# Block-masked attention and a mixture of experts: the row maxima masked in PSUM, the row tails loaded per batch, the token rows stored by two transfers

## Chip, core and metric

The kernel runs on one core of a Trainium2 chip. The metric is the device time of one execution in microseconds (us). The engines are named as in the profile: PE is TensorE (PEld its weight loads), DVE is VectorE, ACT is ScalarE, POOL is GpSimd, SP is SyncE, which here issues most of the DMAs.

## What is computed

```
q, k, v: (8, 8, 576, 64)        # batch, heads, sequence, head dimension
scores = q @ k.T / sqrt(64)
scores = where(pos_q // 64 >= pos_k // 64, scores, -1e9)
attn   = softmax(scores)         # row maximum taken off first, 1e-9 added to the sum
x      = (attn @ v) as (4608, 512)
# router: cosine of x with 8 expert vectors, divided by tau; argmax picks the expert
out[i] = gate[i] * (relu(x[i] @ w1[e]) @ w2[e])      # e = expert of token i
```

The mask is by blocks of 64: a query of block b sees keys of blocks 0 to b.

## The kernel before

**Two stages.** The first 410 us or so are attention with the routing of each batch beside it. The rest is the experts: 36 to 43 slots of 128 tokens, gathered from a DRAM buffer `xbuf`, each through two layers with split (high and low) fp32r products. The change touches the first stage alone.

**Attention by pairs.** Work goes by pairs of heads: 8 batches of 4 pairs, 32 pairs. The two heads of a pair lie on partitions 0 to 63 and 64 to 127. For each pair there are generators of small steps: `prep` (turn q and k on PE, split them into high and low parts on ACT and DVE), `maxes` (row maxima of the scores), `scores` (the scores again, keys on the partitions, then exp), `values` (attention times v, and the sums), `finish` (turn back, divide, write `xrow`), `route` (the router of a whole batch) and `loads` (DMAs three pairs ahead).

**What sets the order.** Nothing is scheduled by the compiler: `run` reads a string for each pair and advances one generator by one step for each letter (`m` maxes, `s` scores, `v` values, `f` finish, `p` prep, `r` route, `l` loads). `FIRST` has the strings of pairs 0 to 4, `FINAL` those of pairs 27 to 31, `STEADY` the one string of the 22 pairs between. Each engine then runs its own instructions in exactly that order.

**The row maxima.** `maxes` takes the queries in five chunks `c` of 128, shifted by 64, so that the lower 64 partitions hold block 2c-1 and the upper 64 block 2c. For each chunk and head one matmul (L326) writes the scores of all keys that the chunk may see into a buffer of the PSUM pool `ps_m` (four buffers, shared by the two heads of `maxes`, by `scores` and by a few small users). DVE then reduces them. As the last 64 keys are seen by the upper half alone, there are two reductions: L332 on 128 partitions over the keys that both halves see, L334 on the upper 64 partitions over the last 64 keys. Chunk 4 is cut in two. L336 takes the least of the (negated) partial maxima, PE turns it (L296, `nmr`), ACT copies it (L342) and SP writes it as a row of `qa` (L344), from where `scores` adds it by a matmul with `ka`.

**Loads and stores.** `load_rows` fills a buffer of 5 x 128 rows for a pair: one DMA for each head's 512 full rows and one for the last 64 rows of both heads (L204). `route` stores the finished rows of a batch to `xbuf` with five DMAs, one for each block of 128 (L593), and for the last two batches through `store`.

Of the kernel before, what the change touches and what calls it, by code (L numbers as in the profile page):

```python
# [18 lines left out]


FIRST = (
    "rmrrmmrmmmmrmsmmpprmrmrmrrmmkrsssmsrrpprrmrmrspsmrmvlssssmrmsrvmvrspmvvvmrsmrkmsssvsmrmvrkssssvrsprpmmvsmrmrmmvpsvmrrm",
    "srfrrmslfrfrprrrmsrprfmfsmmrrvrvprrrsrrrvmrrrvmrmmrpmmrrvvrpmrvvrlr",
    "vmpsfrvrrmrvrrrrrsrmrrrsmmrmrvsfrpmrrsffmrmpsrrrssmrmpfrrsprfssmmvvmrssmmssvmvvmmmrsrsvvvsmpsvmsmvvrrplmsv",
    "msrmrrrfsrrrrrrrfpmrffsrmmprrmrrmrsffsmrrrsvrmmrpvsvrrmmvrprrsrrf",
    "mmsmrprrmsvsrvvrrvmsmmpvrssrrsrrrvrvrmmvrrmsrrmrfmsfrfrlrrsmsfrrpsrrrsrpfsmpfmss",
)
# [3 lines left out]
FINAL = (
    "vrvvvmmmmmrppvvvpvsmsrmmspvrvmsrrsrmvmrrsrrrrrsrmmmvrsffrrrsfmrsmrrrprsrmmmsmsrffsrm",
    "srlvfrrmvvmmrrmmrrmrvvrmvrmmrsvrpsmvrsmrmpmmvrrsrpvvrssmrrspvmmrsmrmrfrfrsrpfffrpsrsssvfsrrsmmmvvvvlsmlpvsvl",
    "rmvpsvmmpmssrsmrvvrrmsmvfspmrsrfffsrfmmmvrmpvmmrrrssrrrrmprsmmmvmrrssvvmrvrvmvmvmrsmrsrsrvmmmfrsvmrsmsv",
    "rrfprlrmsfmsmrmfsmmfsmffrsssvrrsvvvrvsfrrrrrvvssrf",
    "rrssrvrsrrrrsrvsvvrsrrrvrrrrrsssffrsfrrrsfsrsfrrrffrrr",
)


# [9 lines left out]
def kernel(  # L49
# [145 lines left out]
    psum_t = psum.enter_context(ExitStack())  # L195
    ps_t = pool(psum_t, "ps_t", 1, space=PSUM)

    nat = [[op.tile([P, NJ, 2, D], F32, name=f"{nm}n{i}") for nm in "qk"] for i in range(2)]
    vo = [rt.tile([P, NJ, 2, D], F32, name=f"vo{i}") for i in range(NV)]

    def load_rows(a, src, b, h0):
        for hh in range(2):
            nc.sync.dma_start(a[:, 0:NJ - 1, hh, :], src[b, h0 + hh, 0:S - 64, :].rearrange("(j p) d -> p j d", p=P))
        nc.sync.dma_start(a[0:64, NJ - 1, :, :], src[b, h0:h0 + 2, S - 64:S, :].rearrange("h p d -> p h d"))  # L204

    def load(n):
# [59 lines left out]
    en = const.tile([E, 1], F32, name="en")
# [1134 lines left out]
```

## Time and profile before

| What | us |
|---|---|
| median of three timed runs | 872.85 (871.83 to 873.13) |
| the profiled execution | 872.06 |
| its span, first to last instruction | 870.3 |
| PE busy | 834.4 (96%) |
| DVE busy | 685.9 (79%) |
| ACT busy | 419.6 (48%) |
| POOL busy | 442.0 (51%) |

The shares are means over both stages. Matmuls are pipelined and a matmul that waits for its buffer can still count as busy, so that PE's 96% is not a share of useful work. In the expert stage PE is busy without a break; in attention both PE and DVE are busy most of the time.

### The profile page before, as it was taken

The numbers are of one execution on the slowest core, as the hardware profiler recorded it, in microseconds if no ns is written. First come the engines' busy times: TensorE is split into PE (matmuls) and PEld (weight loads), VectorE is DVE, ScalarE is ACT, GpSimd is POOL, SyncE is SP. The second block draws the span as 40 slices with busy tenths as digits, with TensorE's granted clock in tenths as the row PEclk, the third lists the DMA queues.
The fourth block names the chain that finished last, engine by engine and source line by source line (L and its number), as shares of the span: only waits on it lengthen the run. The fifth ranks groups of instructions, "written<-read, shape, count | busy, mean of one in ns | idle before, by whom it ended". The sixth has DMA issues, their size and how long they took to land. (4 is left out here: it accounts for less than half of the span.)

```text
span 870.3 us, 23939 instructions
## 1 busy us (share of the span) xinstructions
PE 834.4 (96%) x7147; PEld 650.0 (75%) x7147; DVE 685.9 (79%) x1829; ACT 419.6 (48%) x991; POOL 442.0 (51%) x509
## 2 busy tenths in 40 slices
PE   8998999999999999999999999999999999999997
PEld 3666776677767766767787888778888888888885
DVE  6787888888888888885886777887777777788772
ACT  2445646556565655566555535554453333442332
POOL 5345465664667465747332837878383111472111
PEclk8799999999999999999999999999999999999999
DMA  3542454343524343331756444745353111012111
GB/s 86 116 115 59 98 134 100 110 110 90 133 60 123 84 128 73 87 77 61 263 190 214 145 147 147 210 150 182 113 163 131 50 51 51 27 46 64 43 40 48
DMA packets 142995, 94.02 MB, mean 108 GB/s; under 512 B 119981, under 2 KB 121597, under 8 KB 142828
## 3 DMA queue, kind: packets, MB, share of 16 engines
q1 hardware_dynamic: 135372, 71.84, 29.6%
q0 software_dynamic: 7456, 20.26, 7.3%
q8 instruction: 67, 1.10, 0.5%
q14 instruction: 100, 0.82, 0.3%
HBM read 72.71 MB, written 19.71 MB: 106 GB/s over the span
## 5 line engine op out<-in xcount | busy, mean ns | idle before, releaser
L1061 DVE STREAM_TRANSPOSE pt<-h 32x256 f32<-32x256 f32 x528 | 240.8, 456 | 18.3 <-ACT h L1033 0.3
L378 ACT ACTIVATE pT<-psm 128x288 f32<-128x288 f32 (+3 forms) x320 | 122.4, 432 | 89.3 <-PE psm L370 83.8
L332 DVE TENSOR_REDUCE nmx<-psm 128x1 f32<-128x320 f32 (+4 forms) x320 | 130.2, 422 | 37.7 <-PE psm L326 31.2
L815 POOL TENSOR_TENSOR ring_l<-raw,ring_h 128x1024 f32 (+1 forms) x49 | 116.4, 2408 | 36.0 <-ACT ring_h L810 18.4
L1075 POOL DMA_INDIRECT out_dram<-y,outi x36 | 37.2, 1034 | 176.9 <-ACTq L964 129.9
L355 POOL TENSOR_TENSOR pS<-pT 128x448 f32<-128x448 f32 x62 | 69.5, 1146 | 96.9 <-ACT pT L378 82.2
L370 PE MATMUL psm<-qh,kh 64*128 64x288 f32 (+4 forms) x384 | 97.0, 344 | 16.6 <-DVE nmx L334 14.3
L355 POOL TENSOR_TENSOR pS<-pS,pT 128x320 f32<-128x320 f32 (+1 forms) x186 | 106.6, 592 | 11.1 <-ACT pT L378 6.1
L1013 PE MATMUL py<-ring_h,hh 128*128 x272 | 109.5, 402 | 0.8 <-ACT hh L1067 0.8
L1013 PE MATMUL ph<-ring_l,xh 128*128 x280 | 109.1, 390 | 1.1 <-POOLq L976 1.1
L1013 PE MATMUL ph<-ring_h,xh 128*128 x280 | 109.1, 390 | 0.6 <-ACTq L964 0.6
L1013 PE MATMUL py<-ring_l,hh 128*128 x272 | 106.3, 391 | 0.0
L404 PE MATMUL psb<-pT,vo 128*64 128x256 f32 (+1 forms) x868 | 104.5, 367 | 0.3 <-DVE lgh L477 0.3
L1033 ACT ACTIVATE h<-ph 128x512 f32<-128x512 f32 x70 | 42.5, 608 | 99.4 <-DVE pt L1061 61.7
L1013 PE MATMUL py<-ring_h,hl 128*128 x272 | 88.8, 389 | 0.0
L1069 DVE TENSOR_TENSOR hl<-pt,hh 128x512 fp32r<-128x512 f32 x66 | 42.5, 687 | 57.6 <-ACT hh L1067 54.2
L370 PEld LDWEIGHTS psm<-qh,kh 64*128 64x128 f32 x384 | 54.8, 189 | 39.5 <-PE psm L326 21.1
L326 PE MATMUL psm<-kh,qh 64*128 64x320 f32 (+4 forms) x384 | 77.8, 354 | 4.5 <-DVE nmx L334 3.7
L334 DVE TENSOR_REDUCE nmx<-psm 64x1 f32<-64x64 f32 x320 | 71.9, 227 | 9.8 <-PE psb L296 3.8
L370 PE MATMUL psm<-ql,kh 64*128 64x288 f32 (+4 forms) x384 | 79.2, 321 | 0.0
L1013 PE MATMUL ph<-ring_h,xl 128*128 x280 | 74.9, 389 | 0.0
L404 PEld LDWEIGHTS psb<-pT,vo 128*64 128x64 f32 x868 | 53.8, 136 | 28.2 <-issue 9.8
(271 smaller groups left out, 1714.9 us busy)
## 6 DMA issues: line engine op xcount, KB each, us to landing
raw<-in_moe_w_dram SPq DMA_DIRECT2D x64, 512.0 KB
qn<-in_q_dram SPq DMA_DIRECT2D x64, 128.0 KB
kn<-in_k_dram SPq DMA_DIRECT2D x64, 128.0 KB
vo<-in_v_dram SPq DMA_DIRECT2D x64, 128.0 KB
xbuf<-xrow SPq DMA_DIRECT2D x24, 260.0 KB
xbuf<-xrow SPq DMA_DIRECT2D x1, 1040.0 KB
qn<-in_q_dram SPq DMA_DIRECT2D x32, 32.0 KB
kn<-in_k_dram SPq DMA_DIRECT2D x32, 32.0 KB
```

The costliest lines, as they stand in the source:

```text
L326: nc.tensor.matmul(mx[hh][:, 0:e - a], qh[i][hd[hh], c * P:(c + 1) * P], kh[i][hd[hh], a:e], start=True, stop=True)
L332: nc.vector.tensor_reduce(m[:, r, u:u + 1], mx[hh][:, 0:w], axis=AX.X, op=ALU.max, negate=True)
L334: nc.vector.tensor_reduce(m[64:P, r, 1:2], mx[hh][64:P, w:e - a], axis=AX.X, op=ALU.max, negate=True)
L355: nc.gpsimd.tensor_tensor(o, pT[0:r, P:S] if t == 1 else o, pT[0:r, off[t]:off[t] + w], op=ALU.add)
L370: nc.tensor.matmul(st[hh][:, o:o + c1 - c0], kk[hd[hh], t * P:(t + 1) * P], qq[hd[hh], 64 + c0:64 + c1], start=(x == 0), stop=(x == len(te ...
L378: nc.scalar.activation(pT[:, f:f + o], st[hh][:, 0:o], AF.Exp, scale=scale)
L404: m = nc.tensor.matmul(ob[hh * D:(hh + 1) * D, b0:b0 + q1 - c0], a[:, t, hh, :], pTs[hh][0][:, f0:f0 + q1 - c0], start=(t == 0), stop=(t = ...
L815: return eng.tensor_tensor(piece(ring_l, to, c, half), raw[i][:, c * CW:(c + 1) * CW], piece(ring_h, to, c, half).bitcast(F32), op=ALU.sub ...
L1013: m = nc.tensor.matmul(out, ac, slots[g]["w", i](r, c * n + off), start=(u == 0 and c == 0), stop=(c == nk - 1 and u == len(turns) - 1))
L1033: nc.scalar.activation(h[:, f:f + 512], ph, AF.Relu)
L1061: nc.vector.transpose(pt[32 * j:32 * j + 32, :, 32 * i:32 * i + 32], h[32 * i:32 * i + 32, :, j, :])
L1069: nc.vector.tensor_tensor(sets["hl"][u], pt[:, 4 * u:4 * u + 4], sets["hh"][u].bitcast(F32), op=ALU.subtract)
```

## The change

It has three parts, and new strings for all pairs. In `maxes`, after the two score matmuls of a chunk, two matmuls of 64 columns (a constant tile `mk`) add -1e30 to the lower 64 partitions in the last 64 columns. One reduction of 128 partitions over all columns then stands for L332 and L334. The last 64 rows of q, k and v of all eight heads of a batch are loaded by one DMA each into tiles of their own (`ends_n`, `ends_v`, two of each). The rows of every batch are stored by `store`, with two DMAs. With the tail tiles zeroed on all 128 partitions, POOL's sum of the last block runs on 128 partitions.

```
 STEADY = (
-    "vvrvvmmmmvvmrpmpmsvsvmmsvsmrsspvmmvmrmmsvfmmrprlfrssfsmssfrpsmfmssrpf",
+    "vrvvvmmmmvvrmmpmspsvmmvspvmmlrsvvsmsrvmrsfmmrmmmffprssssfrsspmfmssrfp",
...
-    def load_rows(a, src, b, h0):
+    def load_rows(a, end, src, n):
+        b, h0 = n // NP, 2 * (n % NP)
+        if h0 == 0:
+            nc.sync.dma_start(end[b % 2][0:64], src[b, :, S - 64:S, :].rearrange("h p d -> p h d"))
         for hh in range(2):
-            nc.sync.dma_start(a[:, 0:NJ - 1, hh, :], src[b, h0 + hh, 0:S - 64, :].rearrange("(j p) d -> p j d", p=P))
-        nc.sync.dma_start(a[0:64, NJ - 1, :, :], src[b, h0:h0 + 2, S - 64:S, :].rearrange("h p d -> p h d"))
+            nc.sync.dma_start(a[:, :, hh, :], src[b, h0 + hh, 0:S - 64, :].rearrange("(j p) d -> p j d", p=P))
...
+    def init_mk(eng):
+        eng.memset(mk.bitcast(F32), 0.0)
+        for g in range(2):
+            eng.memset(mk[g * D:g * D + 1, 0:64].bitcast(F32), 1.0)
+            eng.memset(mk[g * D:g * D + 1, P:P + 64].bitcast(F32), -1.0e30)
...
                 nc.tensor.matmul(mx[hh][:, 0:e - a], qh[i][hd[hh], c * P:(c + 1) * P], kh[i][hd[hh], a:e],
-                                 start=True, stop=True)
+                                 start=True, stop=e <= 2 * c * 64 or c == 0)
+            if e > 2 * c * 64 and c > 0:
+                for hh in range(2):
+                    nc.tensor.matmul(mx[hh][:, e - a - 64:e - a], mk[hd[hh], 0:P], mk[hd[hh], P:P + 64], start=False, stop=True)
             yield "fine"
             for hh in range(2):
-                r, w, u = hh * NJ + c, min(e, 2 * c * 64) - a, 2 if a else 0
-                if w > 0:
-                    nc.vector.tensor_reduce(m[:, r, u:u + 1], mx[hh][:, 0:w], axis=AX.X, op=ALU.max, negate=True)
-                if a + w < e:
-                    nc.vector.tensor_reduce(m[64:P, r, 1:2], mx[hh][64:P, w:e - a], axis=AX.X, op=ALU.max, negate=True)
+                r, u = hh * NJ + c, 1 if a else 0
+                nc.vector.tensor_reduce(m[:, r, u:u + 1], mx[hh][:, 0:e - a], axis=AX.X, op=ALU.max, negate=True)
...
-        if b < B - 2:
-            for j in range(NJ):
-                r0 = b * S + 1 + j * P
-                r = min(P, S - j * P)
-                nc.sync.dma_start(xbuf[r0:r0 + r, :], xrow[0:r, j, :])
-                yield
-        else:
-            store(b, xrow, 0 if b < B - 1 else (NP - 1) * P, RW)
-            yield
+        store(b, xrow, 0 if b < B - 1 else (NP - 1) * P, RW)
+        yield
```

**DVE in a middle pair.** The rows go from the reductions ahead of `ql` (the low part of the next q) to the last reductions of the pair; `rin` and `xrow` are the division of the pair before. Before:

```order
L332 TENSOR_REDUCE nmx_193<-psm 128x1
L334 TENSOR_REDUCE nmx_193<-psm 64x1
L316 TENSOR_TENSOR ql_180<-pst,qh_177 128x2x5x64
L332 TENSOR_REDUCE nmx_193<-psm 128x1
L334 TENSOR_REDUCE nmx_193<-psm 64x1
...
L334 TENSOR_REDUCE nmx_193<-psm 64x1 x2
L464 TENSOR_SCALAR rin<-psb 128x4x2
L466 TENSOR_SCALAR rin<-psb 128x2
L467 RECIPROCAL rin<-rin 128x5x2
L334 TENSOR_REDUCE nmx_193<-psm 64x1
L470 TENSOR_TENSOR xrow<-psb,rin 128x5x128
```

Now:

```order
L351 TENSOR_REDUCE nmx_199<-psm 128x1 x6
L333 TENSOR_TENSOR ql_186<-pst,qh_183 128x2x5x64
L351 TENSOR_REDUCE nmx_199<-psm 128x1 x6
L481 TENSOR_SCALAR rin<-psb 128x4x2
L483 TENSOR_SCALAR rin<-psb 128x2
L484 RECIPROCAL rin<-rin 128x5x2
L487 TENSOR_TENSOR xrow<-psb,rin 128x5x128
```

Twelve reductions stand where there were twenty, and the last of them has moved ahead of `rin`.

**PE in a middle pair,** from the 448-key chunk to the 320-key chunk, with the scores of 288 columns (`kh`, `kl`, `ka`) between. Before:

```order
L326 MATMUL psm<-kh_182,qh_176 128x448 x2
L370 MATMUL psm<-qh_178,kh_184 128x288 x2
L370 MATMUL psm<-ql_181,kh_184 128x288 x2
L370 MATMUL psm<-qh_178,kl_187 128x288 x2
L370 MATMUL psm<-qa_190,ka 128x288 x2
L404 MATMUL psb<-pT,vo_157 64x192 x2
L404 MATMUL psb<-pT,vo_157 64x64 x2
L370 MATMUL psm<-qh_178,kh_184 128x288 x2
...
L326 MATMUL psm<-kh_182,qh_176 128x320 x2
```

Now:

```order
L343 MATMUL psm<-kh_188,qh_182 128x448 x2
L347 MATMUL psm<-mk 128x64 x2
L387 MATMUL psm<-qh_184,kh_190 128x288 x2
...
L421 MATMUL psb<-pT,vo_157 64x192 x2
L421 MATMUL psb<-pT,ve_165 64x64 x2
L343 MATMUL psm<-kh_188,qh_182 128x320 x2
L347 MATMUL psm<-mk 128x64 x2
L387 MATMUL psm<-qh_184,kh_190 128x288 x2
```

The 320-key chunk has moved ahead of the second group of scores; each of four chunks has a pair of `mk` matmuls behind it; the rest of the pair stands as before.

**PE in the first pair,** where the maxima of pair 1 (`kh_183`, now `kh_189`) meet the scores of pair 0. Before:

```order
L326 MATMUL psm<-kh_183,qh_177 128x320 x2
L326 MATMUL psm<-kh_183,qh_177 128x256 x2
L326 MATMUL psm<-kh_183,qh_177 128x448 x2
L370 MATMUL psm<-qh_176,kh_182 128x288 x2
...
L326 MATMUL psm<-kh_183,qh_177 128x320 x2
L296 MATMUL pst<-ident,qn_153 128x64 x10
L326 MATMUL psm<-kh_183,qh_177 128x192 x2
```

Now:

```order
L343 MATMUL psm<-kh_189,qh_183 128x448 x2
L347 MATMUL psm<-mk 128x64 x2
L343 MATMUL psm<-kh_189,qh_183 128x320 x2
L347 MATMUL psm<-mk 128x64 x2
L343 MATMUL psm<-kh_189,qh_183 128x192 x2
...
L343 MATMUL psm<-kh_189,qh_183 128x64 x2
L387 MATMUL psm<-qh_182,kh_188 128x288 x2
```

All chunks of pair 1 now stand ahead of the first scores of pair 0.

## Rows read from the trace of the kernel before

**Rows 1.** Page, part 1: busy us, share of the span, instructions

```profile
PE 834.4 (96%) x7147; PEld 650.0 (75%) x7147; DVE 685.9 (79%) x1829; ACT 419.6 (48%) x991; POOL 442.0 (51%) x509
```

**Rows 2.** Windows: length, busy by engine (x count), PE clock, DMA share, GB/s

```profile
3.00:6.00 3.00, 3.00 (x17) 1.14 (x15) 1.07 (x2) 0.35 (x1) 1.06 (x7) 1.00 0.59 131
...
12.00:15.00 3.00, 1.96 (x6) 1.13 (x6) 2.79 (x12) 0.00 (x0) 2.87 (x5) 0.77 0.00 0
...
18.00:21.00 3.00, 2.63 (x16) 1.22 (x12) 1.84 (x4) 0.69 (x1) 0.00 (x0) 0.50 0.47 108
...
30.00:33.00 3.00, 2.99 (x26) 1.80 (x27) 1.08 (x3) 2.20 (x7) 2.09 (x2) 0.89 0.01 2
...
103.00:301.00 198.00, 187.29 (x2525) 138.84 (x2527) 168.65 (x544) 113.63 (x320) 118.73 (x172) 1.00 0.42 105
```

**Rows 3.** One line's instructions, 103 to 301: count, ns, first and last start

```profile
L444 ACT COPY su<-psb x17: 319/319/325, 103.4 to 300.5; 128x192 f32<-128x192 f32 x17
```

**Rows 4.** Waits, 103 to 301: who <- whom, total us, times, longest

```profile
PEld psm L370 <- PE psm L326: 13.3, 33, 0.5
DVE nmx L332 <- PE psm L326: 11.8, 16, 1.1
PE psm L370 <- DVE nmx L334: 8.8, 34, 0.5
...
PEld psm L370 <- PE psm L370: 5.3, 12, 0.5
...
PEld psm L370 <- PE psm L541: 2.5, 4, 0.6
```

**Rows 5.** Groups by shape, DVE reductions: busy us, mean ns, idle before

```profile
L334 DVE TENSOR_REDUCE nmx<-psm 64x1 f32<-64x64 f32 x320 | 71.9, 227 | 9.8 <-PE psb L296 3.8 <-PE psm L326 0.9 <-PE psm L370 0.3
...
L332 DVE TENSOR_REDUCE nmx<-psm 128x1 f32<-128x384 f32 x64 | 35.7, 558 | 3.1 <-PE psm L326 1.2
...
L332 DVE TENSOR_REDUCE nmx<-psm 128x1 f32<-128x320 f32 x64 | 28.5, 487 | 24.6 <-PE psm L326 24.5
L332 DVE TENSOR_REDUCE nmx<-psm 128x1 f32<-128x256 f32 x64 | 26.9, 421 | 3.9 <-PE psm L326 2.7
...
L332 DVE TENSOR_REDUCE nmx<-psm 128x1 f32<-128x192 f32 x64 | 22.6, 353 | 3.8 <-PE psm L326 2.8
...
L332 DVE TENSOR_REDUCE nmx<-psm 128x1 f32<-128x128 f32 x64 | 18.6, 290 | 2.3 <-PE psm L370 0.4
```

**Rows 6.** Timeline of one middle pair: start, us, instruction [idle before <- releaser]

```profile
188.26 0.23 DVE L334 TENSOR_REDUCE nmx<-psm 64x1 f32<-64x64 f32 x1
188.52 0.42 DVE L332 TENSOR_REDUCE nmx<-psm 128x1 f32<-128x256 f32 x1
...
193.84 0.17 DVE L336 TENSOR_REDUCE nmr<-nmx 128x10 f32<-128x30 f32 x1
...
195.71 0.53 PE L326 MATMUL psm<-kh,qh 64*128 64x320 f32 x4
...
196.15 1.15 DVE L332 TENSOR_REDUCE nmx<-psm 128x1 f32<-128x320 f32 x3 [0.98 <-PE psm L326]
...
197.73 0.45 PE L326 MATMUL psm<-kh,qh 64*128 64x448 f32 x2
```

**Rows 7.** Timeline, same pair: pairs of 64-column matmuls behind one another

```profile
193.61 0.24 PE L370 MATMUL psm<-qh,kh 64*128 64x64 f32 x2
193.66 0.31 PE L370 MATMUL psm<-ql,kh 64*128 64x64 f32 x2
193.77 0.31 PE L370 MATMUL psm<-qh,kl 64*128 64x64 f32 x2
193.88 0.31 PE L370 MATMUL psm<-qa,ka 64*128 64x64 f32 x2
```

**Rows 8.** Timeline of the start: the first turn of k

```profile
6.48 0.64 PE L296 MATMUL psb<-ident,kn 64*128 64x64 f32 x10
```

More of the change, by code (lines that the diff above doesn't have):

```diff
@@ L21 @@
 FIRST = (
[L22 to L26, printed above, removed]
+    "mmmrmmmmmmmmmmpmmmrrrrlmprrsmmpmrkrskrrsrsssprspsssvpmssrrmvvvmkpsmrvsvsrmrvmrvpprvmmmlmvmvmsmvpfmrfssmmrrsmpmsfrsssssffsrrvvsmpsmpmmrrrmrvvpsv",
+    "rpmrrrsmmmvvrrrrrvmvmsmrrsrmvmssmmrrprssrvfrr",
+    "rlrmmrrvprmsrmsrfmfmmfsrprmsrprmrssssrmfprfvrrrrvvsrmvrrprmrvmrsmrsr",
+    "fsvsrmrrsmvmmvrmsmpmvsrrmrrpvrvsvprmrlrrmrssffmrrrsmspsrfffmmrrvsmrsrvfmmvmrmvrpvmvmssprmrrrrvvrrss",
+    "mvrrrrmrrrrrrlrrmvrsrrvmmrsrvmsfmmfrsmrrrmrrprffrfrsrpssrsrsrspsf",
 )
 STEADY = (
-    "vvrvvmmmmvvmrpmpmsvsvmmsvsmrsspvmmvmrmmsvfmmrprlfrssfsmssfrpsmfmssrpf",
+    "vrvvvmmmmvvrmmpmspsvmmvspvmmlrsvvsmsrvmrsfmmrmmmffprssssfrsspmfmssrfp",
 )
 FINAL = (
[L32 to L36, printed above, removed]
+    "vmmvrvvprmmvmvmrpvvvrpmsppmrmrprsvvvslssrrsrrrfrrfsfmfsmrmrmfrsmrmrrsssmmmvmsrmmrmrvprsmsmrpvmrmmvmvvvrvmmvssvvrmsrmrrsvs",
+    "frfrfrssprfrrrfmpmrsrrmssmfvvprmmsrmrslrrpvsprrmrrrrpmfrrmvrvsmsrvvvmrrrmsvsmsr",
+    "mrrvrrrmrvrsvffrmspsmmrrsfmrpsssffsmmmmpvvmmmsvsmrmrvrv",
+    "mrmmrmmssrrvvrvsvrsrlpsmf",
+    "rmmvfmmlmrrvssrssvrrrmsmmfrsmfmmmmfsffrsfssssrrvvfrvvvvvrvsrrrrslsvsrsssrvvsrrrrrsrrvsfsffrsssrrfsfrffr",
 )
@@ L196, with rows @@
     ps_t = pool(psum_t, "ps_t", 1, space=PSUM)
-    nat = [[op.tile([P, NJ, 2, D], F32, name=f"{nm}n{i}") for nm in "qk"] for i in range(2)]
-    vo = [rt.tile([P, NJ, 2, D], F32, name=f"vo{i}") for i in range(NV)]
-    def load_rows(a, src, b, h0):
+    nat = [[op.tile([P, NJ - 1, 2, D], F32, name=f"{nm}n{i}") for nm in "qk"] for i in range(2)]
+    vo = [rt.tile([P, NJ - 1, 2, D], F32, name=f"vo{i}") for i in range(NV)]
+    ends_n = [[op.tile([P, H, D], F32, name=f"{nm}e{i}") for nm in "qk"] for i in range(2)]
+    ends_v = [rt.tile([P, H, D], F32, name=f"ve{i}") for i in range(2)]
+    def load_rows(a, end, src, n):
+        b, h0 = n // NP, 2 * (n % NP)
+        if h0 == 0:
+            nc.sync.dma_start(end[b % 2][0:64], src[b, :, S - 64:S, :].rearrange("h p d -> p h d"))
         for hh in range(2):
-            nc.sync.dma_start(a[:, 0:NJ - 1, hh, :], src[b, h0 + hh, 0:S - 64, :].rearrange("(j p) d -> p j d", p=P))
-        nc.sync.dma_start(a[0:64, NJ - 1, :, :], src[b, h0:h0 + 2, S - 64:S, :].rearrange("h p d -> p h d"))
+            nc.sync.dma_start(a[:, :, hh, :], src[b, h0 + hh, 0:S - 64, :].rearrange("(j p) d -> p j d", p=P))
+    def rows(a, end, n, j):
+        return a[n % len(a)][:, j] if j < NJ - 1 else end[n // NP % 2][:, 2 * (n % NP):2 * (n % NP) + 2]
     def load(n):
-        for a, src in zip(nat[n % 2], (q, k)):
-            load_rows(a, src, n // NP, 2 * (n % NP))
+        for u, src in enumerate((q, k)):
+            load_rows(nat[n % 2][u], [e[u] for e in ends_n], src, n)
     def load_v(n):
-        load_rows(vo[n % NV], v, n // NP, 2 * (n % NP))
+        load_rows(vo[n % NV], ends_v, v, n)
     ctx.enter_context(tc.manual_schedule())
@@ L216 @@
     for i in range(2):
-        for a in nat[i]:
-            nc.gpsimd.memset(a[64:P, NJ - 1], 0.0)
+        for a in ends_n[i]:
+            nc.gpsimd.memset(a[64:P], 0.0)
     exf = xpool.tile([P, NJ, RW], F32, name="xrow").rearrange("p j w -> p (j w)")[0:NJ + 1, 0:2 * SP]
@@ L235 @@
     NB = S // 64
-    nmx = [rt.tile([P, 2 * NJ, 3], F32, name=f"nmx{i}") for i in range(2)]
+    nmx = [rt.tile([P, 2 * NJ, 2], F32, name=f"nmx{i}") for i in range(2)]
+    mk = op.tile([P, P + 64], F32R, name="mk")
     nmr = [rt.tile([P, P], F32, name=f"nmr{i}") for i in range(2)]
@@ L261, in zeros @@
         nc.gpsimd.memset(enT, 0.0)
-        for i in range(NV):
-            nc.gpsimd.memset(vo[i][64:P, NJ - 1], 0.0)
+        for i in range(2):
+            nc.gpsimd.memset(ends_v[i][64:P], 0.0)
     enT = rt.tile([P, NP, 32], F32, name="enT")
@@ L306, in prep @@
             for j in range(NJ):
-                halves_turned(lambda g: pt[:, g * 512 + j * 64:g * 512 + j * 64 + 64], nat[n % 2][u][:, j, :, :])
+                halves_turned(lambda g: pt[:, g * 512 + j * 64:g * 512 + j * 64 + 64],
+                             rows([a[u] for a in nat], [e[u] for e in ends_n], n, j).rearrange("p h d -> p (h d)"))
             yield "fine"
@@ L351, in add @@
     def add(ps, t, pT):
-        r, w = (P if t < NJ - 1 else 64), S - P * t
-        o = ps[0:r, P * (t - 1):S - P]
-        nc.gpsimd.tensor_tensor(o, pT[0:r, P:S] if t == 1 else o, pT[0:r, off[t]:off[t] + w], op=ALU.add)
+        w = S - P * t
+        o = ps[:, P * (t - 1):S - P]
+        nc.gpsimd.tensor_tensor(o, pT[:, P:S] if t == 1 else o, pT[:, off[t]:off[t] + w], op=ALU.add)
     def scores(n):
@@ L391, in values @@
         pTs = made[n]
-        a, o = vo[n % NV], oe[n % 2]
+        o = oe[n % 2]
         ob = ps_b.tile([P, 1024], F32, name="psb") if n < NPAIR - 1 else ps_t.tile([P, 1024], F32, name="pst")
@@ L403, in values @@
                     f0 = off[t] + c0 - t * P
-                    m = nc.tensor.matmul(ob[hh * D:(hh + 1) * D, b0:b0 + q1 - c0], a[:, t, hh, :],
+                    m = nc.tensor.matmul(ob[hh * D:(hh + 1) * D, b0:b0 + q1 - c0], rows(vo, ends_v, n, t)[:, hh, :],
                                          pTs[hh][0][:, f0:f0 + q1 - c0], start=(t == 0), stop=(t == last))
@@ L719 @@
     init(nc.vector, 0)
+    init_mk(nc.vector)
     init_a(nc.vector, ka)
```

## The prediction, made before the changed kernel was run

> **What bounds the kernel now.** I read the page's busy line first: PE 96%, DVE 79% [rows 1]. Both are means over two stages, and the change touches attention alone, so I took the windows next. In the 198 us of even attention from 103 to 301, PE is busy 187.29 and DVE 168.65 [rows 2]. Seventeen copies of one kind, one for each pair, start from 103.4 to 300.5 [rows 3]: 197.1 us over 16 intervals, 12.32 us for a pair, in which DVE works 168.65 / 16.07 = 10.5 us. To see which of the two waits for the other I read the waits of the same stretch [rows 4]. PE's matmuls of the scores wait for reductions of L334 34 times, 8.8 us. That counts only the time in which no earlier matmul is still shown as running. The weight loads in front of those matmuls stand still longer: 13.3 us behind a chunk of maxima (L326), 5.3 behind scores and 2.5 behind the routing, each time since the pool's next PSUM buffer has not yet been reduced. Together that is 21.1 us, or 21.1 / 16 = 1.32 us a pair. DVE in turn waits for PE 16 times, 11.8 us, once a pair, for the first chunk of the next pair.
>
> The timeline shows the loop that these make [rows 6]. DVE ends the maxima with L336 at 193.84; PE turns the result, does the values it has queued, and only then the next first chunk (195.71), whose reduction starts at 196.15. That is 2.31 us from L336 to the first reduction. The remaining 12.32 - 2.31 = 10.01 us DVE is at work nearly without a pause. So in attention DVE sets the pace over most of a pair and PE over the rest.
>
> **The change, part by part.**
>
> *Reductions.* In a pair L334 runs ten times (x320 for 32 pairs), 227 ns each [rows 5], and 0.26 us from its start to the next one's start (188.26 to 188.52) [rows 6]. Two of the ten (chunk 0) stay, as 128 x 64. Eight go, and the reductions beside them become 64 columns wider. From 256 to 320 columns that costs 487 - 421 = 66 ns, from 320 to 384 it costs 71, from 128 to 192 it costs 63 [rows 5]; I take 67. The relief is 8 x (0.26 - 0.067) = 1.54 us of DVE a pair, or 8 x (0.227 - 0.067) = 1.28 if the gap behind an instruction is kept.
>
> [...]
>
> *Mask matmuls.* Four chunks each get two matmuls of 64 columns, one for each half of the rows. Such pairs stand in the scores of the last key block: starts 193.66, 193.77, 193.88 [rows 7], 0.11 us for a pair of them. They have the tile form of the chunks (64 rows, 128 columns), so I take that price: 4 x 0.11 = 0.44 us of PE a pair. From below the bound is 0.05 (the start at 193.61 to the next at 193.66), from above 0.11 plus nothing that a row shows.
>
> [...]
>
> *What a pair gains.* I work it out in two ways. By the waits: the 1.32 us that PE stands still for DVE's buffers go, since each buffer is held shorter, and 0.44 is paid: 0.88. By the loop: DVE's 10.01 becomes 10.01 - 1.54 = 8.47, plus 2.31 is 10.78. But DVE now gets ahead of PE at one place. The three reductions that begin at 196.15 end at 197.30; in the new order all four of chunk 4 end about 1.64 us after 196.15, at 197.79. The 448-key chunk stands behind values and the turning of q on PE and comes out at 197.73 + 0.45 [rows 6], 0.11 later with its mask: 198.29. So DVE is idle there for 0.5 us: 11.28, a gain of 1.04. I take 0.96 between the two.
>
> *Steady and edge pairs.* The order of the 22 middle pairs is nearly the old one: the 320-key chunk ahead of the second group of scores, and the reduction of chunk 0 ahead of `rin` instead of behind it (it held back the scores of the last two key blocks). So the full gain stands for 22 pairs: 21.1 us. The ten pairs of the first and last strings are ordered quite differently now; I take half, 4.8 us, with 0 and 9.6 as ends.
>
> *Tails.* Bytes are the same over a batch, so the DMA share of 0.42 [rows 2] stays. SP issues six loads a pair instead of nine, plus three a batch. The tails of q and k now stand ahead of the first rows: 2 x 96 KB more before the first k is complete. At 131 GB/s [rows 2] that is 1.5 us at most; nothing, if the filling matmuls ahead of the first turn of k (6.48 [rows 8]) cover it. I take 0.7 us.
>
> *Stores, zeros, constants.* Two stores a batch for five. On SP the pair of stores now stands ahead of the next `qa` row, which scores wait for. The gate that the store needs is written by DVE ahead of the pair's last reductions, and the row only after them, so the store does not hold it: 0. The memsets of `mk` fall where DVE is busy 1.07 of 3 us [rows 2]. POOL's last sum on 128 partitions hides in POOL's 118.73 of 198.
>
> *The sum.* 21.1 + 4.8 - 0.7 = 25.2 us off the profiled execution's 872.06: 846.9. The median of the runs is 0.8 above that execution, so I forecast 847.7.
>
> **The rivals.**
>
> *DVE's loop alone.* If PE is always ready, the 0.5 us of new idle does not come: 1.54 a pair, 22 x 1.54 + 10 x 0.77 - 0.7 = 40.9, 832 us. For it: DVE's only wait in [rows 4] is the one a pair. Against: PE needs its own time for values and turns between chunks.
>
> *The buffers take it back.* Four PSUM buffers are two pairs of them. With the 320-key chunk moved ahead, it must wait until the 448-key chunk is reduced, which comes behind a chunk 0.5 us late. If half of the 1.32 us comes back in this way, a pair gains 0.66 - 0.44 = 0.22: 5.9 - 0.7 = 5.2 us, 867.6. If a little more comes back, the time is unchanged.
>
> *PE is the bound (slower).* PE is shown as busy 95% of even attention. If the idle weight loads are covered by matmuls still streaming, then taking DVE's work away frees nothing and eight more matmuls a pair are simply added: 32 x 0.44 = 14.1, with the start 887.6. It decides where less than 0.44 us of PE's waits goes for a pair. The 8.8 us of idle matmul time are only 0.55 us a pair, so it is not far; against it speaks that DVE has 10.5 of 12.32 us of work and that the buffers are held by it.
>
> [...]
>
> **How the numbers follow.** Forecast 0.50; DVE's loop alone 0.10; the buffers 0.18; PE the bound 0.12; the clock 0.05; no change, where gain and price meet, 0.05. A measurement of this kernel tells about 0.2% (1.7 us) from no change. Faster: 0.50 + 0.10 + 0.05 and all but 0.01 of the buffers, 0.82. Within 0.2%: 0.06. Slower: 0.12. The range reaches up to the buffers' 868 and down to 833, which takes in half of DVE's loop alone (its edge pairs gain anything from 0 to all); 0.17 is left out.
>
> **What would show it.** In the profile after: 12 reductions a pair, 128 x 448 near 0.62 us; DVE busy near 9.2 us a pair; the distance from pair to pair 11.2 to 11.5 us; PE's waits on DVE down to a third; `mk` matmuls 0.11 us a pair of them; a short wait of DVE for the 448-key chunk; the expert stage as before. It is wrong if the pair is above 12 us, if the wait in front of the 320-key chunk is long, or if the first pairs take longer than before.

## The result, and the profile after

The changed kernel takes 840.26 us in the median of four runs (837.98 to 841.55), the kernel before on the same chip 872.99 (871.83 to 873.22). The ratio is 0.9625, with an interval of 0.9602 to 0.9648: 32.7 us or 3.7% faster. The forecast was 847.7, with 833 to 868 as its range; sign and mechanism held, the gain is 7.4 us larger than forecast. The profiled execution takes 839.99 us and spans 838.3.

Part 1 of the page, as in [rows 1] (busy us, share of the span, instructions):

```profile
PE 821.3 (98%) x7403; PEld 658.0 (78%) x7403; DVE 621.7 (74%) x1578; ACT 413.8 (49%) x991; POOL 443.4 (53%) x507
```

PE has 256 instructions more (the masks) and yet 13 us less busy time. The busy time of before holds waiting too: PE was busy 187.29 / (198 / 12.32) = 11.65 us a pair in even attention [rows 2], and in the kernel without masks (below) it is 161.44 / (162 / 10.79) = 10.75 us, with the same matmuls. DVE has 251 instructions and 64 us less.

The share that decides is that of even attention. The windows of after (length, busy by engine, PE clock, DMA share, GB/s), the first to be held against the last row of [rows 2], the others against its start:

```profile
103.00:270.00 167.00, 166.88 (x2506) 132.03 (x2502) 126.13 (x389) 102.05 (x294) 114.18 (x166) 1.00 0.48 119
3.00:6.00 3.00, 2.22 (x15) 0.79 (x13) 1.56 (x6) 0.00 (x0) 2.34 (x7) 1.00 0.96 209
6.00:9.00 3.00, 1.96 (x21) 0.76 (x16) 0.82 (x1) 1.38 (x2) 0.91 (x2) 0.93 0.95 202
9.00:12.00 3.00, 3.00 (x12) 1.93 (x12) 1.65 (x4) 0.00 (x0) 2.75 (x5) 0.50 0.05 6
```

PE is busy 166.88 of 167 us, and DVE 126.13, 76% (85% before). Per pair DVE is busy 126.13 / (167 / 11.04) = 8.3 us instead of 10.5. The pace has passed from DVE to PE. PE's share alone would not show that, since PE counted as busy for some 0.9 us a pair more before (11.65 for 10.75); the waits do, and so do the masks added twice below (0.43 and 0.39 us a pair).

The waits of the same stretch (engine and line <- what it waited for: us, times, longest), to be held against [rows 4]:

```profile
DVE nmx L351 <- PE psm L347: 17.0, 30, 0.9
...
DVE nmx L351 <- PE psm L343: 14.4, 26, 1.2
...
PEld psm L343 <- ACT oe L427: 5.4, 11, 0.5
PEld pst L312 <- DVE nmx L351: 3.9, 8, 0.5
```

The waits of PE and its weight loads for psm buffers that DVE had not yet reduced (8.8, 13.3 and 5.3 us) are gone from the list. The rows of the 13.3 and 5.3 us name PE as what ended them; that DVE's reductions stood behind them is read from their going away here and with the masked reductions alone. DVE now waits for PE 31.4 us, at 56 places instead of 16.

The reductions by shape (busy us, mean ns | idle before them), as in [rows 5]:

```profile
L351 DVE TENSOR_REDUCE nmx<-psm 128x1 f32<-128x320 f32 x128 | 56.7, 483 | 24.9 <-PE psm L343 20.8 <-PE psm L347 4.1
L351 DVE TENSOR_REDUCE nmx<-psm 128x1 f32<-128x448 f32 x64 | 37.0, 619 | 13.7 <-PE psm L347 13.7
...
L351 DVE TENSOR_REDUCE nmx<-psm 128x1 f32<-128x64 f32 x64 | 11.7, 220 | 12.5 <-PE psm L343 12.2 <-PE psm L387 0.2
```

And all of them together, of after:

```profile
L351 DVE TENSOR_REDUCE nmx<-psm 128x1 f32<-128x320 f32 (+4 forms) x384 | 147.4, 429 | 72.1 <-PE psm L347 38.6 <-PE psm L343 33.0 <-PE psm L387 0.2
```

and of before:

```profile
L332 DVE TENSOR_REDUCE nmx<-psm 128x1 f32<-128x320 f32 (+4 forms) x320 | 130.2, 422 | 37.7 <-PE psm L326 31.2 <-PE psm L370 0.4
...
L334 DVE TENSOR_REDUCE nmx<-psm 64x1 f32<-64x64 f32 x320 | 71.9, 227 | 9.8 <-PE psb L296 3.8 <-PE psm L326 0.9 <-PE psm L370 0.3
```

202.1 us became 147.4: the time in which DVE is at a reduction is 1.71 us less for a pair. Added up by count and mean duration the reductions are only 1.34 us shorter; the rest is that neighbouring wide reductions overlap in the records (384 x 429 ns is 164.7 us, and they fill 147.4).

The copy `su` runs once a pair, as in [rows 3] (count, ns, first and last start):

```profile
L461 ACT COPY su<-psb x32: 298/319/342, 39.2 to 384.3; 128x192 f32<-128x192 f32 x32
```

These copies cut the span into pieces. Numbered from 0, with the 22 middle pairs between copies 4 and 26:

| Piece of the span, us | before | after | difference |
|---|---|---|---|
| start to copy 0 | 42.1 | 39.2 | -2.9 |
| copies 0 to 4 | 48.2 | 46.1 | -2.1 |
| copies 4 to 26 (22 pairs) | 271.9 | 242.6 | -29.3 |
| copies 26 to 31 | 56.6 | 56.4 | -0.2 |
| copy 31 to the end (routing's rest, experts) | 451.4 | 454.0 | +2.6 |
| one pair of even attention (16 intervals) | 12.32 | 11.04 | -1.28 |

Two pieces are not as forecast: a middle pair gained 1.33 us instead of 0.96, and the expert stage, which the change does not touch, became longer.

### The profile page after: what moved, and what is told of

Read it like the earlier page. It is cut to its first block, busy times and chain, and to the rows that moved or that the text cites. A ratio compares the mean times of both kernels' runs of the same rounds, so it can differ in the third digit from the quotient of the medians.

```text
span 838.3 us, 23780 instructions
## 1 busy us (share of the span) xinstructions
PE 821.3 (98%) x7403; PEld 658.0 (78%) x7403; DVE 621.7 (74%) x1578; ACT 413.8 (49%) x991; POOL 443.4 (53%) x507
## 5 line engine op out<-in xcount | busy, mean ns | idle before, releaser
L351 DVE TENSOR_REDUCE nmx<-psm 128x1 f32<-128x320 f32 (+4 forms) x384 | 147.4, 429 | 72.1 <-PE psm L347 38.6
L421 PE MATMUL psb<-pT,vo 128*64 128x256 f32 (+1 forms) x744 | 101.0, 393 | 0.1
L387 PE MATMUL psm<-qh,kh 64*128 64x288 f32 (+4 forms) x384 | 78.1, 353 | 0.6 <-ACT nmT L359 0.2
L343 PE MATMUL psm<-kh,qh 64*128 64x320 f32 (+4 forms) x384 | 76.1, 373 | 2.0 <-ACT pT L395 1.1
L821 ACT CAST ring_h<-raw 128x1024 f32 (+1 forms) x62 | 60.9, 1047 | 29.5 <-SPq L994 13.6
L1085 ACT ACTIVATE y<-py,xg 128x512 f32<-128x512 f32 x34 | 23.4, 688 | 100.4 <-PE py L1024 96.5
L387 PE MATMUL psm<-ql,kh 64*128 64x288 f32 (+4 forms) x384 | 67.4, 306 | 0.0
L387 PE MATMUL psm<-qh,kl 64*128 64x288 f32 (+4 forms) x384 | 66.2, 303 | 0.0
```

What stands on the lines that cost most here:

```text
L351: nc.vector.tensor_reduce(m[:, r, u:u + 1], mx[hh][:, 0:e - a], axis=AX.X, op=ALU.max, negate=True)
L387: nc.tensor.matmul(st[hh][:, o:o + c1 - c0], kk[hd[hh], t * P:(t + 1) * P], qq[hd[hh], 64 + c0:64 + c1], start=(x == 0), stop=(x == len(te ...
L821: return (nc.scalar.copy if eng is nc.scalar else eng.tensor_copy)(piece(ring_h, to, c, half), raw[i][:, c * CW:(c + 1) * CW])
```

## Experiments

Twelve kernels ran in three sets, each set with runs of the kernel before on the same chip; all ratios are to these. In the second set (the kernels with the old load, the doubled masks, the split first tails and the tails alone) every kernel, that of before too, took some 50 us longer, by a stall in each batch that is described at the end; there the text compares ratios and the pairs that the stall leaves alone. The pieces in the text are those of the table above.

### Which part brings the gain

**The masked reductions alone,** in the kernel before: old strings, loads and stores.

```
+            if e > 2 * c * 64 and c > 0:
+                for hh in range(2):
+                    nc.tensor.matmul(mx[hh][:, e - a - 64:e - a], mk[hd[hh], 0:P], mk[hd[hh], P:P + 64], start=False, stop=True)
...
-                if w > 0:
-                    nc.vector.tensor_reduce(m[:, r, u:u + 1], mx[hh][:, 0:w], axis=AX.X, op=ALU.max, negate=True)
-                if a + w < e:
-                    nc.vector.tensor_reduce(m[64:P, r, 1:2], mx[hh][64:P, w:e - a], axis=AX.X, op=ALU.max, negate=True)
+                nc.vector.tensor_reduce(m[:, r, u:u + 1], mx[hh][:, 0:e - a], axis=AX.X, op=ALU.max, negate=True)
```

> The kernel before with the masked reductions alone; its own strings, loads and stores. Theory 1 (DVE's relief is the cause, the order matters little): the pair falls to about 11.3 us and the time to 843 to 850. Theory 2 (the new order is needed to use the relief): PE still waits for buffers at the old places, the pair stays at 11.8 to 12.1 and the time is 858 to 868. Theory 3 (PE's extra matmuls are paid in full where the order is old): 873 or more.

Measured: 837.23 us, ratio 0.9614 (0.9579 to 0.965); a pair takes 11.12 us. Its window of even attention:

```profile
103.00:270.00 167.00, 167.00 (x2492) 133.25 (x2488) 124.61 (x385) 103.50 (x294) 112.53 (x164) 1.00 0.47 118
```

PE is busy without a break here too, and the waits of [rows 4] for unreduced `psm` buffers are gone from its list. The whole gain of the change is there without the strings, the loads and the stores.

**All but the masked reductions:** the changed kernel with the two reductions of before.

```
-                nc.vector.tensor_reduce(m[:, r, u:u + 1], mx[hh][:, 0:e - a], axis=AX.X, op=ALU.max, negate=True)
+                if w > 0:
+                    nc.vector.tensor_reduce(m[:, r, u:u + 1], mx[hh][:, 0:w], axis=AX.X, op=ALU.max, negate=True)
+                if a + w < e:
+                    nc.vector.tensor_reduce(m[64:P, r, 1:2], mx[hh][64:P, w:e - a], axis=AX.X, op=ALU.max, negate=True)
```

> The changed kernel with the two reductions of before in place of the masked one; new strings, loads and stores stay. Theory 1: DVE has its old work again, the pair is 12.2 to 12.6 us, the time 870 to 885. Theory 2: the new strings alone bring 8 to 15 us, 858 to 865.

Measured: 868.91 us, ratio 0.9965 (0.9944 to 0.9985). An even pair gains 0.53 us from the new string (11.79 for 12.32), but copies 0 to 4 lose 3.8 us and copies 26 to 31 lose 5.3: the new edge strings do not suit the longer reductions, and the granted clock is 0.50 in part of both pieces (from 44.5 to 48.0 and from 358.6 to 365.4 us). The result fits neither theory: the pair is shorter than the first one has it, and the time is longer than the second one's.

**The old strings** in the changed kernel:

```
 STEADY = (
-    "vrvvvmmmmvvrmmpmspsvmmvspvmmlrsvvsmsrvmrsfmmrmmmffprssssfrsspmfmssrfp",
+    "vvrvvmmmmvvmrpmpmsvsvmmsvsmrsspvmmvmrmmsvfmmrprlfrssfsmssfrpsmfmssrpf",
 )
```

(`FIRST` and `FINAL` likewise.)

> The changed kernel with the strings of before. With the masked reductions alone it tells what loads and stores add, with the changed kernel what the strings add. Theory 1: the strings are worth 3 to 8 us, 843 to 848. Theory 2: the strings are worth 15 or more, 855 to 870.

Measured: 842.71 us, ratio 0.9681 (0.9648 to 0.9714), a pair 11.11 us against 11.04. With the masked reductions in place the strings bring 0.07 us a pair, and by the medians some 3 us in all; the 0.53 of the kernel without them does not add to the gain. Both remove some of the same waits. With the new strings and the old reductions the waits from 103 to 290 have

```profile
PEld psm L387 <- PE psm L343: 9.5, 31, 0.4
...
PE psm L343 <- DVE nmx L351: 1.2, 4, 0.3
```

PE's matmul waits for reductions, 8.8 us in [rows 4], are down to 1.2; most of the weight loads' wait behind the maxima, 13.3 us there, is still here. It takes the masked reductions to remove that.

**DVE's load given back:** the changed kernel, with a reduction of the old size beside each wide one, into a column that nothing reads.

```
                 nc.vector.tensor_reduce(m[:, r, u:u + 1], mx[hh][:, 0:e - a], axis=AX.X, op=ALU.max, negate=True)
+                if e > 2 * c * 64 and c > 0:
+                    nc.vector.tensor_reduce(spare[64:P], mx[hh][64:P, e - a - 64:e - a], axis=AX.X, op=ALU.max, negate=True)
```

> The changed kernel with its masks, and behind each of the eight masked reductions of a pair the old 64 x 64 reduction again, into a spare column that nobody reads. PE's work is as in the changed kernel, DVE's is 2.1 us a pair more than there. If DVE's load is the cause: the pair goes back to 12.3 us or beyond (the masks are still paid), the time to 868 to 885. If the number of buffer hand-overs or the place of the masks made the gain: the pair stays below 11.6 us, under 855.

Measured: 931.33 us, ratio 1.0142 (1.0066 to 1.0218). The copies `su` of one batch (start, us, instruction, idle before):

```profile
153.67 0.32 ACT L464 COPY su<-psb 128x192 f32<-128x192 f32 x1 [0.24 <-PE psb L462]
166.99 0.32 ACT L464 COPY su<-psb 128x192 f32<-128x192 f32 x1
178.93 0.32 ACT L464 COPY su<-psb 128x192 f32<-128x192 f32 x1
```

those of the same two pairs of a batch in the changed kernel:

```profile
129.47 0.32 ACT L461 COPY su<-psb 128x192 f32<-128x192 f32 x1 [0.33 <-PE psb L459]
141.10 0.34 ACT L461 COPY su<-psb 128x192 f32<-128x192 f32 x1
151.88 0.32 ACT L461 COPY su<-psb 128x192 f32<-128x192 f32 x1 [0.20 <-PE psb L459]
```

and in the kernel before:

```profile
90.27 0.32 ACT L444 COPY su<-psb 128x192 f32<-128x192 f32 x1 [0.37 <-PE psb L442]
103.39 0.32 ACT L444 COPY su<-psb 128x192 f32<-128x192 f32 x1
115.33 0.32 ACT L444 COPY su<-psb 128x192 f32<-128x192 f32 x1 [0.25 <-PE psb L442]
```

The pairs take 13.32 and 11.94 us for 11.63 and 10.78; in the kernel before they take 13.12 and 11.94, and the same in the kernel of this set with the tails alone. The gain is gone, with PE's work unchanged. The load is somewhat more than the old one, since the wide reductions stay wide: some 0.5 us of reductions a pair (8 x 67 ns, the step of the prediction).

This kernel and the first one together show the cause in both directions: taking the reductions away alone brings the gain, and putting them back (with that excess) removes it.

### What the masks cost

**No masks:** the changed kernel without the `mk` matmuls. It takes the maxima over 64 keys more than it should for the lower half; the maximum only shifts the exponent.

```
-                                 start=True, stop=e <= 2 * c * 64 or c == 0)
-            if e > 2 * c * 64 and c > 0:
-                for hh in range(2):
-                    nc.tensor.matmul(mx[hh][:, e - a - 64:e - a], mk[hd[hh], 0:P], mk[hd[hh], P:P + 64], start=False, stop=True)
+                                 start=True, stop=True)
```

> The changed kernel without the mask matmuls: the maximum of the lower 64 rows then runs over 64 keys more than they see, and the shift by it cancels in the division. If PE sets the pace of the changed kernel and a pair of mask matmuls takes 0.11 us: 0.44 us a pair less, 14 us, 826. If the masks hide in PE's waits: 836 to 840. If waiting DVE for the masks is the price: the pair falls by more than 0.44 us.

Measured: 832.86 us, ratio 0.9548 (0.9507 to 0.9589), a pair 10.79 us. So the masks cost 11.04 - 10.79 = 0.25 us a pair. Its window:

```profile
103.00:265.00 162.00, 161.44 (x2372) 125.39 (x2376) 125.15 (x387) 102.66 (x296) 111.55 (x160) 1.00 0.48 121
```

PE is the pace here too, at 161.44 of 162.

**The masks twice:**

```
-                for hh in range(2):
-                    nc.tensor.matmul(mx[hh][:, e - a - 64:e - a], mk[hd[hh], 0:P], mk[hd[hh], P:P + 64], start=False, stop=True)
+                for last in (False, True):
+                    for hh in range(2):
+                        nc.tensor.matmul(mx[hh][:, e - a - 64:e - a], mk[hd[hh], 0:P], mk[hd[hh], P:P + 64], start=False, stop=last)
```

> The changed kernel with each mask added twice: eight more 64-column matmuls a pair. Without the masks the even pairs took 10.79 us, with them 11.04. If a pair of mask matmuls has one price, the pair goes to 11.29 and the time up by 7 to 9 us, 848. If the first masks were half covered by PE's waits and PE now has none left: 0.44 a pair, 11.48, 854.

Measured: 898.43 us, ratio 0.9772 (0.9702 to 0.9842). The copies of one batch:

```profile
137.75 0.32 ACT L462 COPY su<-psb 128x192 f32<-128x192 f32 x1 [0.34 <-PE psb L460]
149.81 0.32 ACT L462 COPY su<-psb 128x192 f32<-128x192 f32 x1
160.98 0.32 ACT L462 COPY su<-psb 128x192 f32<-128x192 f32 x1 [0.22 <-PE psb L460]
```

12.06 and 11.17 us instead of 11.63 and 10.78: the second masks cost 0.43 and 0.39 us a pair, four times about the 0.11 of [rows 7]. The first cost 0.25, some 60% of that. Why they cost less is not shown: idle time of PE that they could fill does not show in the kernel without masks, where PE stands still 0.56 us in 162, or 0.04 us a pair.

### Loads and the start

**The tails alone,** in the kernel before:

```
-    def load_rows(a, src, b, h0):
+    def load_rows(a, end, src, n):
+        b, h0 = n // NP, 2 * (n % NP)
+        if h0 == 0:
+            nc.sync.dma_start(end[b % 2][0:64], src[b, :, S - 64:S, :].rearrange("h p d -> p h d"))
...
-        nc.sync.dma_start(a[0:64, NJ - 1, :, :], src[b, h0:h0 + 2, S - 64:S, :].rearrange("h p d -> p h d"))
```

> The kernel before with the tails loaded once a batch and nothing else. Theory: fewer loads for SP bring nothing, the larger first loads cost 1.3 to 3.5 us at the start: 873 to 876 beside 871.3 to 873. Rival: SP's shorter issue brings the rows earlier: 868 to 871.

Measured: 917.32 us, ratio 0.9985 (0.9947 to 1.0022), undisturbed pairs 13.12 and 11.95 as before; copy 0 at 42.8 for 42.1. The first turn of k comes at 7.41 instead of 6.48 [rows 8]. The tails are worth nothing that can be measured.

**The first batch's tails in two parts,** in the changed kernel: two heads with pair 0, six with pair 1.

```
-        if h0 == 0:
-            nc.sync.dma_start(end[b % 2][0:64], src[b, :, S - 64:S, :].rearrange("h p d -> p h d"))
+        g0, g1 = (0, 2) if n == 0 else (2, H) if n == 1 else (0, H if h0 == 0 else 0)
+        if g1:
+            nc.sync.dma_start(end[b % 2][0:64, g0:g1], src[b, g0:g1, S - 64:S, :].rearrange("h p d -> p h d"))
```

> The changed kernel, in which the first batch's tails come in two parts: with pair 0 those of its two heads, the other six heads' with pair 1. In the changed kernel the first k was turned at 7.74 us instead of 6.48. If the larger first loads are the price: the first k comes back to about 6.5, the first pair ends 1.3 to 3.5 us earlier, 837 to 839. If the start hides it: no change, 840.

Measured: 886.4 us, ratio 0.9629 (0.9558 to 0.97). The first turn of k, of the changed kernel:

```profile
7.74 0.46 PE L312 MATMUL psb<-ident,kn 64*128 64x64 f32 x8 [1.04 <-DMA kn<-in_k_dram]
```

and of this one:

```profile
6.77 0.47 PE L313 MATMUL psb<-ident,kn 64*128 64x64 f32 x8 [0.36 <-DMA kn<-in_k_dram]
```

0.97 us earlier. Copy 0 comes at 36.7 for 39.2, but that is not all the edit's: the changed kernel itself, run again, has it at 37.1, as told next.

**The changed kernel again,** beside the two that follow:

> The changed kernel once more, beside the other kernels of this group. Its ratio to the kernel before was 0.9625 (0.960 to 0.965); the same is expected, with an even pair of 11.04 us wherever no pair is held up.

Measured: 839.43 us, ratio 0.9616 (0.9578 to 0.9654), a pair 11.04 us, tail 454.3. The start differs: the granted clock is 0.50 from 8.6 to 32.5 us in the first profile of this kernel, and here from 13 to 19.9 and from 23.3 to 30.1, 10 us less in all; copy 0 comes 2.0 us earlier. In the kernel before it was 13.6 to 30.7. The lower clock at the start is thus no fixed property of the kernel, and the table's first line scatters by two us from one execution to another: by this one its difference is -5.0.

### The stores and the expert stage

**Two stores a batch alone,** in the kernel before:

```
-        if b < B - 2:
-            for j in range(NJ):
...
-        else:
-            store(b, xrow, 0 if b < B - 1 else (NP - 1) * P, RW)
-            yield
+        store(b, xrow, 0 if b < B - 1 else (NP - 1) * P, RW)
+        yield
```

> The kernel before with two stores a batch instead of five and nothing else. Theory: nobody on the path waits for the stores; ratio 0.998 to 1.002. Rival: the one large store stands ahead of the row that scores wait for, on the queue of SP, and holds it: 1.003 or more.

Measured: 875.98 us in ten runs, ratio 1.0047 (1.0021 to 1.0074): a little slower. That lies in the rival's range, but not for the rival's reason: attention is as before (pair 12.31, copies 4 to 26 271.7), so nothing waits behind the stores on SP. The loss is in the tail, 454.2 for 451.4. Most of it stands at one place, shortly after the first change of expert, where PE has pauses in the kernel before as well (busy 22.89 of 25 us from 550 to 575). The timeline of PE there in the kernel before:

```profile
561.16 0.50 PE L1013 MATMUL ph<-ring_l,xh 128*128 x1 [1.09 <-POOLq L976]
...
567.69 0.66 PE L997 MATMUL px<-ident,xg 128*128 128x128 f32 x4 [1.02 <-DMA xg<-xbuf,rowi]
568.10 0.47 PE L1013 MATMUL py<-ring_h,hh 128*128 x1
```

and of ACT:

```profile
563.50 2.00 ACT L810 CAST ring_h<-raw 128x1024 f32 x2 [2.93 <-POOLq L976]
```

The same of PE with two stores:

```profile
559.69 0.50 PE L1006 MATMUL ph<-ring_l,xh 128*128 x1 [1.12 <-POOLq L969]
...
565.85 0.66 PE L990 MATMUL px<-ident,xg 128*128 128x128 f32 x4 [0.64 <-DMA xg<-xbuf,rowi]
568.43 0.50 PE L1006 MATMUL py<-ring_h,hh 128*128 x1 [1.93 <-ACT hh L1060]
```

and of ACT:

```profile
565.42 1.99 ACT L803 CAST ring_h<-raw 128x1024 f32 x2 [6.35 <-SPq L976]
```

From PE's `ring_l` matmul to ACT's split of the next weights (`ring_h`) it is 2.34 us before and 5.73 with two stores. ACT waits there for SP's instruction stream (L976, the branch in front of the next weight load), and `h` and `hh` are queued behind the split on ACT; PE stands still for `hh`, 1.93 us, and the second layer starts 8.74 us after the `ring_l` matmul instead of 6.94. In this execution the granted clock then falls to 0.50 as well (window, columns as above):

```profile
570.00:572.00 2.00, 2.00 (x6) 1.54 (x6) 1.90 (x5) 0.53 (x1) 2.00 (x2) 0.50 0.08 27
```

The same wait of ACT for SP, with a wait of PE for `hh` of 0.9 to 1.9 us behind it, stands in eight of the nine profiles of kernels with two stores (the one with the split first tails lacks it, and its tail is 450.7), and in none of the five with five stores. The traces narrow the reason down. At that branch SP steps through four semaphores one after another, and in all fourteen profiles its stream stops among them for 1.1 to 3.5 us. The waits of SP show it, with two stores (556 to 567):

```profile
SPq L976 <- SPq L976: 4.0, 2, 3.6
```

and in the kernel before (560 to 640):

```profile
SPq L983 <- SPq L983: 12.1, 8, 3.1
```

In the kernel before the stop is from 563.50 to 566.57, behind three of the four semaphores, and ACT waits for the first of them, so it has gone on by then. With two stores the stop is from 561.69 to 565.23, and ACT waits for the fourth, behind it. It is the fourth in all eight kernels that have the wait and the first in the six that have not, the one with the split first tails among them. So it is not the stores themselves that hold ACT (the last one to `xbuf` was issued 130 us earlier, at 435.3), but at which of the four semaphores it waits. The kernels differ in how many DMAs SP has issued until then: 437 or 365 with five stores, 419 or 347 with two, 350 with two and the split first tails. That this count sets the order of the semaphores is likely, but not shown. Nor is the reason of the stop; in each of them one or two packets of 8 KB move on the queue that the page calls `q14 instruction`.

### A version without what costs

**The masked reductions and the new `STEADY`,** with all else as before:

```
 STEADY = (
-    "vvrvvmmmmvvmrpmpmsvsvmmsvsmrsspvmmvmrmmsvfmmrprlfrssfsmssfrpsmfmssrpf",
+    "vrvvvmmmmvvrmmpmspsvmmvspvmmlrsvvsmsrvmrsfmmrmmmffprssssfrsspmfmssrfp",
 )
...
+                    nc.tensor.matmul(mx[hh][:, e - a - 64:e - a], mk[hd[hh], 0:P], mk[hd[hh], P:P + 64], start=False, stop=True)
```

> The kernel before with the masked reductions and the new string for the 22 middle pairs alone; its old strings for the first and last pairs, old loads and stores. With old strings throughout, the masked reductions gave a ratio of 0.9614 and 11.12 us a pair; the changed kernel lost 3.3 us at the start to its loads and some 4 at the end. Theory: the middle string takes 0.08 us more off 22 pairs, 1.8 us: ratio 0.959 to 0.961, ahead of the changed kernel. Rival: the middle string fits only between its own edges, and the time is that of the old strings or above, 0.962 or more.

Measured: 834.11 us, ratio 0.9567 (0.952 to 0.9614). A pair takes 11.04 us as in the changed kernel; copies 26 to 31 take 54.1 for 56.4 and the tail 451.4 for 454.3. It keeps the gain and leaves out what costs, 5 us below the changed kernel in the same set (the two intervals overlap a little; the pieces show where the time goes). The 3.3 us at the start that the expectation puts down to the loads are not borne out: the start is 38.4 us here and 37.1 in the changed kernel of this set, and the tails alone moved it by 0.7.

**The same without the masks** (maxima over 64 keys more, as above):

```
+                r, u = hh * NJ + c, 1 if a else 0
+                nc.vector.tensor_reduce(m[:, r, u:u + 1], mx[hh][:, 0:e - a], axis=AX.X, op=ALU.max, negate=True)
```

> The same kernel without the mask matmuls: the maximum of the lower 64 rows runs over 64 keys more than they see, and the shift cancels in the division. Dropping them took 0.25 us off an even pair of the changed kernel (11.04 to 10.79) and 7 us off its time; the same here: ratio 0.950 to 0.953.

Measured: 826.35 us, ratio 0.9471 (0.9431 to 0.9511), a pair 10.79 us. This is the fastest of all, 13 us below the changed kernel in the same set (839.43).

## Why the prediction was right, and where it was off

**The bound** was read rightly: DVE's work held the buffers, and what was lost was the time in which weight loads and matmuls of PE stood behind them. The waits of [rows 4] that the forecast expected to go are gone, and the two kernels on DVE's load show the cause in both directions.

**The relief of DVE** was forecast at 1.54 us a pair (1.28 from below); the reductions show 1.71 by the time that they fill and 1.34 by their durations. DVE's whole work fell to 8.3 us a pair, where the forecast expected 9.2; the overlap of the wide reductions was not in it. Of the single prices, 619 ns for 448 columns, 483 for 320 and 220 for 64 are near those used.

**The gain of a pair** was the term that was mis-sized: 0.96 forecast, 1.33 measured over the 22 middle pairs (1.28 over the 16 even ones), 29.3 us instead of 21.1. Both parts of the waits' route were off in the same direction. The waits removed (and the new string, 0.07 of it) are worth 12.32 - 10.79 = 1.53 us by the kernel without masks, where the list gave 1.32; and the masks cost 0.25, not 0.44. 1.53 - 0.25 is the 1.28 measured. The price of 0.11 us for a pair of mask matmuls is what the doubled masks cost; that the first masks cost only some 60% of it was missed, and the reason stays open.

**The loop's route** gave 11.28 us for a pair, with 0.5 us of new idle of DVE ahead of the 448-key chunk. That idle is there, 13.7 / 32 = 0.43 us a pair in the row of the 448-column reductions. But the pair closed at 11.04: DVE no longer sets it, as it waits for PE 31.4 us in 167 us, 2.1 us a pair. That the 10.79 without masks is so near to the 10.78 that the route gives without the idle is chance: PE is busy 161.44 of 162 in that kernel, and DVE 125.15.

**Edge pairs and start** were forecast at -4.8 + 0.7 = -4.1 us together; they measure -2.9 - 2.1 - 0.2 = -5.2, or -7.3 by the second profile of the changed kernel, with 2 us of scatter in the start. That the sum comes near is in part luck. Within this the parts were not as thought: the last pairs gained 0.2 us only, with 56.4 us, where the old `FINAL` strings with the masked reductions take 54.1 to 54.2; the new ones cost here what they were to bring. The first turn of k came 1.26 us later (7.74 for 6.48), near the bound of 1.5 rather than the 0.7 taken, but no loss of that size shows at copy 0.

**The stores** were costed at 0, for the reason that nothing on SP waits behind them. In attention that holds. The step that failed is "Stores, zeros, constants": the expert stage was to be "as before", and it became 2.6 us longer, through a wait of ACT for SP that nothing in the forecast looked at: ACT's semaphore now comes after a stop in SP's stream that the kernel before has too, but there after ACT's semaphore. In the changed kernel the place of that wait accounts for 1.6 us of it (8.57 for 6.94); where the rest went isn't located.

**The rivals.** *PE is the bound (slower)* fell: the idle weight loads were not covered by matmuls, and freeing them was worth 1.53 us a pair against a price of 0.25. Yet its half was true: PE is the bound of the new kernel (busy 166.88 of 167 us), and matmuls added to it show: 0.43 and 0.39 us a pair for the second masks. *The buffers take it back* fell: no wait of PE for the reduction of a `psm` buffer is left in the list. *DVE's loop alone* fell with PE at 166.88 of 167. *The clock*, with 0.05 of the chances: before, the granted clock is 0.50 for about 17 us of the start (13.6 to 30.7); in the changed kernel it is 0.50 for 23.9 us in one execution and for 14 in another, and copy 0 comes 2.0 us later in the first of these.

**The signs.** Of those that the prediction named, the twelve reductions of a pair, the 620 ns of the widest and the short wait for the 448-key chunk came as said, and PE's waits fell further than said. The pair (11.04) and DVE's work (8.3) lie below what was named, and the expert stage is not as before. The interval from copy 0 to 1 is longer (13.25 us for 10.59), but the first four together are shorter, 46.1 for 48.2.

## What to carry to other kernels

Read who is waited for, in front of the weight loads too, before believing a busy share: PE at 95% here was waiting for DVE for some 1.3 to 1.5 us of 12.3, and DVE, at 85%, was the bound since it held PE's buffers. Where the waits point to one engine, fewer and wider instructions on it can pay even if the other engine gets extra work, as here (12 reductions a pair for 20: 11.12 us for 12.32 by them alone), until that one is full; then even its 64-column matmuls show (0.25 us a pair for the masks, 0.43 and 0.39 for the second ones). Measure the parts of a change apart: the masked reductions brought all the gain, the new middle string a little, and the version without the new edge strings, loads and stores is some 5 us faster than the whole; about 3 of these lie in a stage that the change does not touch.

## What was not expected of the hardware

In the second set of runs all kernels, that of before too (921.64 us for 871.3), stood still once a batch beside four indirect DMAs of POOL. In the kernel with the split first tails, on POOL:

```profile
118.56 0.97 POOL L611 DMA_INDIRECT table<-tokf,rowj  x1 [0.30 <-issue]
121.37 2.23 POOL L373 TENSOR_TENSOR pS<-pT 128x448 f32<-128x448 f32 x2 [1.84 <-ACT pT L396]
```

on ACT:

```profile
120.52 0.32 ACT L462 COPY su<-psb 128x192 f32<-128x192 f32 x1 [4.71 <-remote]
```

and by windows:

```profile
116.00:120.00 4.00, 1.88 (x20) 1.09 (x12) 0.00 (x0) 0.00 (x0) 2.91 (x3) 1.00 0.13 25
120.00:124.00 4.00, 3.10 (x46) 3.06 (x47) 2.69 (x12) 2.11 (x6) 2.56 (x3) 0.78 0.03 4
124.00:128.00 4.00, 4.00 (x26) 2.53 (x27) 1.46 (x2) 1.70 (x6) 3.13 (x6) 0.50 0.01 1
```

DVE and ACT do nothing from 116 to 120 while POOL issues the DMAs; PE runs out of work, and its granted clock is 0.50 in the window after it has started again. In the first and third sets the same DMAs cost no such time. What differs between the sets isn't shown.

In the expert stage of the kernel with two stores alone, PE's 1.93 us of waiting for `hh` was followed by a granted clock of 0.77 and 0.50 in the next two windows of 2 us. At 0.50 the matmuls of the second layer start 0.43 us apart (570.20, 570.63, 571.06), and 0.23 with the clock back at 1.00 (572.65, 572.88, 573.11), so that more was lost there than the 1.93 us. After the changed kernel's 1.42 us at the same place the clock stayed at 1.00 and the matmuls start 0.23 us apart (535.92, 536.15, 536.38). What lowers the clock isn't shown.
